# Linear attention and a token mixer in one kernel: mix columns in token order through a stepped matmul operand, and one 256 KB store for each output tile

## The chip, the core and the metric

The kernel runs on one core of a Trainium2 chip. The metric is the device time of one execution in microseconds (us). Before the change three runs took 142.1, 142.66 and 143.6 us; the median is 142.66.

A core has five engines that run side by side, each with its own list of instructions in a fixed order: TensorE (PE; its weight loads are shown as PEld), VectorE (DVE), ScalarE (ACT), GpSimd (POOL) and SyncE (SP). SP issues most DMAs here and ACT a few; 16 DMA engines move the bytes. PE writes only to PSUM (8 banks of 2 KB in each of 128 partitions), and ACT or DVE copies from there to SBUF. In names such as SPq or ACTq the q stands for the engine's sequencer, which waits and issues DMAs.

## The reference: what is computed

Inputs are q, k, v of shape (8, 8, 576, 64) (batches, heads, tokens, head dimension) and three weights, all float32. A linear attention with cosine and sine weights over the positions gives x of shape (8, 576, 512); a mixer over the tokens then gives the output of shape (8, 576, 512) in float32.

```python
r = np.maximum(x, 0.0); phi = np.concatenate([r * c, r * s], axis=-1)   # q_p, k_p
kv = np.einsum('bhsf,bhsd->bhfd', k_p, v);  z = np.sum(k_p, axis=2)
num = np.einsum('bhsf,bhfd->bhsd', q_p, kv)
den = np.einsum('bhsf,bhf->bhs', q_p, z)[..., None] + 1e-06
x = (num / den)                      # heads side by side: (b, s, 512)
wq = x @ w_q;  wk = x @ w_k          # (b, s, 64)
W_tok = scale * np.einsum('bsd,btd->bst', wq, wk)
mixed = np.einsum('bst,btd->bsd', W_tok, x)
out = np.maximum(mixed, 0.0) @ w_out
```

The kernel takes the mixer in another order: it multiplies wk with x first (kx, 64 x 512 for a batch) and then wq with that (mix), so the 576 x 576 matrix W_tok is never made.

## The kernel before

**Layout.** Tokens of a batch lie in SBUF as 64 rows of 9: token t = 9 s + c is at row s and chunk c, which lets a load read long runs. Two head pairs make a "half batch" H, 16 of them; rows 0 to 63 of a tile hold one head of a pair and rows 64 to 127 the other. Everything that is transposed from such tiles has its 576 columns in the order (c, s): 9 blocks of 64. That is the column order of `xT_buf`, of `wT_buf` (rows 0 to 63 wq, rows 64 to 127 wk, the columns after a first block of 64 zeros) and of `wq2`, a copy of wq on rows 64 to 127.

**Stages.** For each H the loads of q, k and v (L250: each a tile `raw` of 128 x 2 x 576 float32, made of two DMAs of 288 KB, one for each head pair), ReLU and cast on POOL (L350, L375), the weighting of k on DVE (L363), transposes of q and their weighting (L385, L391), kv (L399), the numerator and denominator (L424, L428), the division on DVE (L435, L437). For each batch: transposes of x (L449), wq and wk (L464, copied by `wqk_evac`), `wq2` (L475), kx (L494), then mix: four steps j for a batch. Step j = 2 nh + i takes half nh of the tokens and 128-wide part i of each half of the 512 features; it makes two matmuls (L510, `mx_mm`), r = 0 on rows 0 to 63 against `wT_buf`, r = 1 on rows 64 to 127 against `wq2`, into two banks. `mx_evac` (L522 on ACT, L524 on DVE) scales, applies the ReLU and writes 288 columns of `mix_sb` for both.

**Output.** `mix_sb` holds two batches, 1152 columns. Output tile rt (9 for two batches, 36 in all) multiplies 128 of these columns with w_out in four matmuls (L534, `wout_mm`) and is copied to `o_sb` (L337 on ACT, L339 on DVE), one of ten buffers. As the columns are in the order (c, s), 64 columns share one c, and their tokens lie 9 apart: `store` (L544) therefore sends two DMAs of 64 rows of 2 KB, 18 KB apart in memory. `out_dest` computes where each begins.

**Order of work.** `plan_order` lays every operation out ahead of time from a table of costs: it fixes each engine's order and, for copies, which of ACT and DVE makes them. The change does not touch it. SP issues loads and stores in that one order, so that a store which waits for its copy holds back the loads behind it. For the last two batches the second half of tiles 4 to 8 is issued by ACT instead (L617), behind ACT's own copy of that tile.

Of the kernel before, what the change touches and what calls it, by code (L numbers as in the profile page):

```python
# [181 lines left out]
def kernel(  # L182
# [10 lines left out]
    nc = tc.nc  # L193

    B, NH, S, D = q.shape
    DM = NH * D
    DH = moe_w_q.shape[1]
    P = 128
    NPAIR = NH // 2
    C9 = (2 * S) // P  # L200
# [6 lines left out]
    SLOTS = C9 + 1  # L207
    KW = 2 * (D + 1)
    hs = S // 2
# [15 lines left out]
    def bank(i, n=1):  # L225
        return ps[:, i:i + n, :]
# [13 lines left out]
    def load(H, parts=((0, C9),), names=("q", "k", "v"), engs=()):  # L240
        if H >= NB:
            return
        b, h0 = divmod(2 * H, NPAIR)
        for nm in names:
            raw[nm, H] = inp.tile([P, 2, HC], FP32, name="raw")
        for lo, hi in parts:
            for nm in names:
                eng = nc.scalar if lo == 0 and nm in engs else nc.sync
                for i in range(2) if H else (slice(0, 2),):
                    eng.dma_start(raw[nm, H][:, i, lo * D:hi * D],  # L250
                                  srcs[nm][b][:, h0:h0 + 2, lo * D:hi * D][:, i])
# [48 lines left out]
    v_bufs, rq_bufs, qpt_bufs, xT_bufs, wT_bufs = [], [], [], [], []  # L300
# [20 lines left out]
    def load_w(part):  # L321
        if part == 0:
            nc.sync.dma_start(wq_f, moe_w_q.rearrange("(c p) j -> p c j", p=P))
            nc.sync.dma_start(wk_f, moe_w_k.rearrange("(c p) j -> p c j", p=P))
        else:
            nc.sync.dma_start(wo_f, moe_w_out.rearrange("(c p) n -> p c n", p=P))
# [25 lines left out]
    def relu_q(H, lo, hi, eng):  # L352
        relu(rq_bufs[H % 3][:, lo:hi], raw_c("q", H, lo, hi), eng)

    def relu_k(H, lo, hi, eng):
        if lo == 0:
            rks[H] = prep.tile([P, C9, 2, D], BF16, name="rk")
        relu(rks[H][:, lo:hi], raw_c("k", H, lo, hi), eng)

    def mul_k(H, lo, hi):  # L360
        if lo == 0:
            kp[H] = prep.tile([P, 2 * C9, 2, D], BF16, name="kp")
        nc.vector.tensor_mul(  # L363
            kp[H][:, 2 * lo:2 * hi],
            rks[H][:, lo:hi].rearrange("p c i d -> p (c i) d").unsqueeze(2)
            .to_broadcast([P, 2 * (hi - lo), 2, D]),
            cossin[:, 2 * lo:2 * hi])

    def cast_v(H, lo, hi, eng):
        src = raw_c("v", H, lo, hi)  # L370
        dst = v_bufs[H % 3][:, lo:hi, :, 0:D]
        if eng is nc.scalar:
            nc.scalar.copy(dst, src)
        else:
            eng.tensor_scalar(dst, src, 1.0, 1.0, op0=ALU.mult, op1=ALU.mult)  # L375

    xs, kvs, wkjs, wqTs, kxs, mixs = {}, {}, {}, {}, {}, {}

    def half_rows(r):
        return slice(64 * r, 64 * r + 64)  # L380

    def qT_mm(H):
        for c in range(C9):
            for r in range(2):
                nc.tensor.transpose(  # L385
                    bank_h(K0 + r)[:, 0, c * D:(c + 1) * D],
                    rq_bufs[H % 3][half_rows(r), c, :, :],
                    ident[half_rows(r), half_rows(r)])

    def qT_evac(H, r):  # L390
        nc.vector.tensor_mul(  # L391
            qpt_bufs[H % 2][:, r, :, D:SLOTS * D],
            bank_h(K0 + r)[:, 0:1, 0:HC].to_broadcast([P, 2, HC]), cst)

    def kv_mm(H):
        for c in range(C9):
            for i in range(2):
                for r in range(2):
                    nc.tensor.matmul(  # L399
                        bank(K0 + r)[:, 0, i * (D + 1):(i + 1) * (D + 1)],  # L400
                        kp[H][half_rows(r), 2 * c + i, :, :],
                        v_bufs[H % 3][half_rows(r), c, i, 0:D + 1],
                        start=(c == 0 and i == 0), stop=(c == C9 - 1 and i == 1))

    def kv_evac(H, eng):
        kv_sb = small.tile([P, 2, KW], BF16, name="kv_sb")
        kv_sh = small.tile([P, 2, D + 1], BF16, name="kv_sh")
        src = bank(K0, 2)
        copy(eng, kv_sb, src[:, :, 0:KW])
        copy(eng, kv_sh[0:64], src[64:128, :, 0:D + 1])  # L410
        copy(eng, kv_sh[64:128], src[0:64, :, D + 1:KW])
        kvs[H] = (kv_sb, kv_sh)
# [18 lines left out]
    def norm(H, r):  # L431
        b, h = divmod(H, 2)
        nv = bank(N0, 2)[:, :, 0:SC * (D + 1)].rearrange("p t (u e) -> p t u e", u=SC)
        rec = small.tile([P, 2, SC, 1], FP32, name="rec")
        nc.vector.reciprocal(rec, nv[:, :, :, D:D + 1])  # L435
        xv = xs[b].rearrange("p u (h t r) d -> p h r t u d", h=2, r=2)
        nc.vector.tensor_tensor(  # L437
            xv[:, h, r], nv[:, :, :, 0:D], rec.to_broadcast([P, 2, SC, D]), op=ALU.mult)
# [15 lines left out]
    def xT_evac(H, r, m, eng):  # L454
        b, h = divmod(H, 2)
        xv = xT_bufs[b % 2].rearrange("p m (c s) -> p m c s", s=D)
        n = SC - 1 + r
        copy(eng, xv[:, 2 * h:2 * h + 2, 1 - r:C9:2, :],
             bank_h(m)[:, 0, 0:2 * n * D].rearrange("p (m u s) -> p m u s", m=2, u=n))
# [45 lines left out]
    def mx_mm(b, j, m):  # L505
        nh, i = divmod(j, 2)
        for r in range(2):
            rhs = (wT_bufs[b % 2][0:64, D + nh * hs:D + (nh + 1) * hs] if r == 0
                   else wqTs[b][64:128, nh * hs:(nh + 1) * hs])
            nc.tensor.matmul(  # L510
                bank(m + r)[:, 0, 0:hs], kxs[b][half_rows(r), i * P:(i + 1) * P],
                rhs, start=True, stop=True)
# [10 lines left out]
        else:  # L523
            eng.tensor_scalar(dst, src, scale_moe, 0.0, op0=ALU.mult, op1=ALU.max)  # L524

    def out_dest(bp, rt, hi):
        bloc, j0 = divmod(P * rt + 64 * hi, S)
        return (2 * bp + bloc) * S * DM + (j0 // 64) * DM

    o_sbs = {}  # L530

# [7 lines left out]
        o_sbs[bp, rt] = outpool.tile([P, DM], FP32, name="o_sb")  # L539
        copy(eng, o_sbs[bp, rt], bank(m)[:, 0, :])  # L540

    def store(bp, rt, qs):
        for hi in range(2):
            qs[hi].dma_start(  # L544
                dataclasses.replace(out, offset=out.offset + out_dest(bp, rt, hi),
                                    ap=[[C9 * DM, 64], [1, DM]]),
                o_sbs[bp, rt][64 * hi:64 * hi + 64, :])

    A, V, G = nc.scalar, nc.vector, nc.gpsimd
    engs = {"ACT": A, "DVE": V}  # L550
# [7 lines left out]
    def emit(n, eng, m):  # L558
        kind, b, j = n[0], n[1], n[2] if len(n) > 2 else 0
        if kind == "load":  # L560
            load(j, names=(b,))
        elif kind == "load_w":
            load_w(b)
        elif kind == "rq":
            for lo, hi in CS:
                relu_q(b, lo, hi, G)
        elif kind == "rk":
            for lo, hi in CS:
                relu_k(b, lo, hi, G)
        elif kind == "rv":  # L570
            for lo, hi in CS:
                cast_v(b, lo, hi, G)
        elif kind == "mk":
            mul_k(b, 0, C9)
        elif kind == "qT":
            qT_mm(b)
        elif kind == "qe":
            qT_evac(b, j)
        elif kind == "kv":
            kv_mm(b)  # L580
        elif kind == "kve":
            kv_evac(b, engs[eng])
        elif kind == "num":
            num_mm(b, j)
        elif kind == "norm":
            if b // 2 not in xs:
                xs[b // 2] = xpool.tile([P, SC, NH, D], BF16, name="x_sb")
            norm(b, j)
        elif kind == "xT":
            xT_mm(b, m)  # L590
        elif kind == "xe":
            xT_evac(b, j, m, engs[eng])
        elif kind == "wqk":
            wqk_mm(b, m)
        elif kind == "we":
            wqk_evac(b, m, engs[eng])
        elif kind == "wqc":
            wq_copy(b)
        elif kind == "wk":
            wk_mm(b, m)  # L600
        elif kind == "wke":
            wk_evac(b, m, engs[eng])
        elif kind == "kx":
            kx_mm(b, m)
        elif kind == "kxe":
            kx_evac(b, m, engs[eng])
        elif kind == "mx":
            mx_mm(b, j, m)
        elif kind == "mxe":
            mx_evac(b, j, m, engs[eng])  # L610
        elif kind == "wo":
            wout_mm(b, j, m)
        elif kind == "oe":
            wout_evac(b, j, m, engs[eng])
        elif kind == "st":
            last = b == B // 2 - 1 and j >= 4
            store(b, j, (nc.sync, A if last else nc.sync))  # L617
        elif kind == "cw":
            cast_w(b)
        elif kind == "warm":  # L620
            warm_up(b)
# [33 lines left out]
```

## Time and profile before

| what | us |
|---|---|
| median of three runs | 142.66 |
| the profiled execution, its own time | 143.6 |
| its span, first to last instruction | 141.5 |
| PE busy / DVE / ACT / POOL | 113.6 / 94.5 / 78.7 / 74.7 |
| matmuls of the output, L534, 144 of 413 ns | 40.5 |
| matmuls of mix, L510, 64 of about 0.32 | 18.4 |
| stores issued by SP / by ACT, of 128 KB | 67 / 5 |

The kernel reads 29.62 MB from memory and writes 9.44 MB. "Busy" is time in which an engine works; waiting and issuing are not in it. Matmuls are pipelined, so that the duration of one is longer than its distance from the next: where the text needs what a matmul takes from PE, it uses distances in the chain of waits. That chain follows the work that ended last back from the end of the span: start, length and what it was, each step leading to what released it. The granted clock is the share of full speed that PE's clock had. The DMA share is the mean busy share of the 16 DMA engines, and can be slightly above 1.

### The profile page before, as it was taken

What the parts mean: (1) busy time and instruction counts of PE and PEld (TensorE: products, weight loads), DVE (VectorE), ACT (ScalarE), POOL (GpSimd) and SP (SyncE); (2) the same over time, 40 slices, a digit from 0 to 9 for tenths busy, and PEclk for the clock granted to TensorE, in tenths of its full rate; (3) what the DMA queues carried; (4) which work ended last, traced back from release to release, by engine and by line L of the source; (5) the groups of instructions that cost most, each with busy time, mean ns of one, the idle gap of its engine ahead of it and who ended that gap; (6) DMA issues with size and microseconds to landing.
All of it is one profiled execution on the core that took longest, in us unless ns stands there. A gap on an engine that the chain in (4) does not pass through costs nothing.

```text
span 141.5 us, 5415 instructions
## 1 busy us (share of the span) xinstructions
PE 113.6 (80%) x2279; PEld 65.8 (47%) x2279; DVE 94.5 (67%) x153; ACT 78.7 (56%) x154; POOL 74.7 (53%) x121
## 2 busy tenths in 40 slices
PE   5958668676999899689583999599919999989940
PEld 2325346445556456355352466356516575533310
DVE  1166986989929999885959595869468736454400
ACT  6930165377757766675373487466825535745440
POOL 7638978995999988273375545964370000000000
PEclk9999999997589999999999599959985569999996
DMA  3999999999999999999999999989866031755974
GB/s 105 370 390 390 347 373 390 368 390 393 393 390 381 300 324 285 311 315 251 313 337 356 354 351 339 378 275 281 281 200 155 5 74 34 153 116 129 199 215 129
DMA packets 21960, 39.41 MB, mean 279 GB/s; under 512 B 3760, under 2 KB 5296, under 8 KB 21936
## 3 DMA queue, kind: packets, MB, share of 16 engines
q1 hardware_dynamic: 21264, 38.09, 82.3%
q10 hardware_dynamic: 672, 0.98, 2.4%
q8 instruction: 18, 0.29, 0.9%
q14 instruction: 6, 0.05, 0.1%
HBM read 29.62 MB, written 9.44 MB: 276 GB/s over the span
## 4 chain that ended last, share of the span: by engine, by line
DMA 57%; PE 15%; SPq 6%; DVE 6%; POOL 5%; issue 3%; ACT 3%; ACTq 2%; POOLq 0%
DMA raw<-in_k_dram 20%; DMA raw<-in_q_dram 18%; DMA raw<-in_v_dram 8%; DMA out_dram<-o_sb 7%; PE ps L534 7%; SPq L250 5%; DMA wq_f<-in_moe_w_q_dram 4%; POOL rk L350 3%; ACT o_sb L337 2%; DVE qpt_buf L391 2%; PE ps L464 2%; DVE kp L363 2%; ACTq L544 2%; PE ps L424 1%; PE ps L399 1%
## 5 line engine op out<-in xcount | busy, mean ns | idle before, releaser
L534 PE MATMUL ps<-wo_sb,mix_sb 128*128 128x512 bf16 x144 | 40.5, 413 | 0.7 <-ACT o_sb L337 0.5
L363 DVE TENSOR_TENSOR kp<-rk,cossin 128x2304 bf16<-128x2304 bf16 (+2 forms) x17 | 22.4, 1318 | 18.7 <-POOL rk L350 12.7
L375 POOL TENSOR_SCALAR v_buf<-raw 128x640 bf16<-128x640 f32 (+1 forms) x30 | 25.6, 869 | 11.1 <-DMA raw<-in_v_dram 7.8
L350 POOL TENSOR_SCALAR rq_buf<-raw 128x640 bf16<-128x640 f32 (+1 forms) x32 | 25.5, 813 | 10.7 <-DMA raw<-in_q_dram 9.3
L337 ACT COPY o_sb<-ps 128x512 f32<-128x512 f32 x32 | 18.8, 587 | 20.7 <-PE ps L534 13.3
L437 DVE TENSOR_TENSOR x_sb<-ps,rec 128x640 bf16<-128x640 f32 x32 | 26.4, 825 | 1.1
L424 PE MATMUL ps<-kv_sb,qpt_buf 64*128 64x65 bf16 x320 | 16.8, 198 | 10.9 <-DVE x_sb L437 10.8
L424 PEld LDWEIGHTS <-qpt_buf 64*128 64x128 bf16 x640 | 15.0, 98 | 21.3 <-issue 20.2
L350 POOL TENSOR_SCALAR rk<-raw 128x640 bf16<-128x640 f32 (+1 forms) x30 | 19.6, 671 | 9.0 <-DMA raw<-in_k_dram 7.3
L391 DVE TENSOR_TENSOR qpt_buf<-ps,cst 128x1152 bf16<-128x1152 bf16 x32 | 22.6, 748 | 0.0
L534 PEld LDWEIGHTS <-mix_sb 128*128 128x128 bf16 x144 | 12.4, 102 | 15.7 <-issue 5.2
L522 ACT ACTIVATE mix_sb<-ps 128x576 bf16<-128x576 f32 x24 | 14.7, 660 | 6.0 <-PE ps L510 6.0
L399 PE MATMUL ps<-v_buf,kp 64*128 64x65 bf16 x576 | 15.1, 203 | 3.6 <-DVE qpt_buf L391 2.5
L337 ACT COPY xT_buf<-ps 128x640 bf16<-128x640 bf16 (+1 forms) x25 | 15.7, 650 | 3.4 <-PE ps L449 2.2
L424 PE MATMUL ps<-kv_sh,qpt_buf 64*128 64x65 bf16 x320 | 16.8, 197 | 0.9
L399 PEld LDWEIGHTS <-kp 64*128 64x128 bf16 x576 | 12.2, 102 | 8.7 <-issue 3.7
L337 ACT CAST kv_sb<-ps 128x260 bf16<-128x260 f32 x13 | 4.9, 377 | 13.6 <-PE ps L399 13.1
L260 PE MATMUL ps<-warm 128*128 128x512 bf16 x31 | 10.2, 472 | 1.5 <-DVE warm L256 1.5
L510 PE MATMUL ps<-wT_buf,kx 64*128 64x288 bf16 x32 | 9.1, 319 | 2.2 <-ACT mix_sb L522 1.6
L435 DVE RECIPROCAL rec<-ps 128x10 f32<-128x10 f32 x32 | 6.9, 215 | 5.8 <-PE ps L428 5.5
L510 PE MATMUL ps<-wq,kx 64*128 64x288 bf16 x32 | 9.3, 321 | 1.1 <-DVE wq L475 0.8
L464 PE MATMUL ps<-xT_buf,wqk_sb 128*128 128x288 bf16 x64 | 9.9, 301 | 0.0
(51 smaller groups left out, 117.1 us busy)
## 6 DMA issues: line engine op xcount, KB each, us to landing
raw<-in_q_dram SPq DMA_DIRECT2D x30, 288.0 KB, 5.9
raw<-in_k_dram SPq DMA_DIRECT2D x30, 288.0 KB, 5.6
raw<-in_v_dram SPq DMA_DIRECT2D x30, 288.0 KB, 5.6
out_dram<-o_sb SPq DMA_DIRECT2D x67, 128.0 KB, 4.1
wo_f<-in_moe_w_out_dram SPq DMA_DIRECT2D x1, 1024.0 KB, 8.1
out_dram<-o_sb ACTq DMA_DIRECT2D x5, 128.0 KB, 2.8
raw<-in_k_dram ACTq DMA_DIRECT2D x1, 320.0 KB, 4.4
raw<-in_q_dram SPq DMA_DIRECT2D x1, 320.0 KB, 4.1
```

The lines of the kernel that those rows point to most:

```text
L337: nc.scalar.copy(dst, src)
L350: eng.tensor_scalar(dst, src, FMAX, 0.0, op0=ALU.min, op1=ALU.max)
L363: nc.vector.tensor_mul(kp[H][:, 2 * lo:2 * hi], rks[H][:, lo:hi].rearrange("p c i d -> p (c i) d").unsqueeze(2) .to_broadcast([P, 2 * (hi ...
L375: eng.tensor_scalar(dst, src, 1.0, 1.0, op0=ALU.mult, op1=ALU.mult)
L391: nc.vector.tensor_mul(qpt_bufs[H % 2][:, r, :, D:SLOTS * D], bank_h(K0 + r)[:, 0:1, 0:HC].to_broadcast([P, 2, HC]), cst)
L399: nc.tensor.matmul(bank(K0 + r)[:, 0, i * (D + 1):(i + 1) * (D + 1)], kp[H][half_rows(r), 2 * c + i, :, :], v_bufs[H % 3][half_rows(r), c, ...
L424: nc.tensor.matmul(nb[t][:, u, :], qpt_bufs[H % 2][rows, r, w, u * P:(u + 1) * P], mv, start=(u == 0 and w == 0), stop=False)
L437: nc.vector.tensor_tensor(xv[:, h, r], nv[:, :, :, 0:D], rec.to_broadcast([P, 2, SC, D]), op=ALU.mult)
L464: nc.tensor.matmul(bank(m + nh)[:, 0, 0:hs], wqk_sb[:, dmc, :, :], xT_bufs[b % 2][:, dmc, nh * hs:(nh + 1) * hs], start=(dmc == 0), stop=( ...
L510: nc.tensor.matmul(bank(m + r)[:, 0, 0:hs], kxs[b][half_rows(r), i * P:(i + 1) * P], rhs, start=True, stop=True)
L522: nc.scalar.activation(dst, src, AF.Relu, scale=scale_moe)
L534: nc.tensor.matmul(bank(m)[:, 0, :], mixs[bp][:, dmc, rt * P:(rt + 1) * P], wo_sb[:, dmc, :], start=(dmc == 0), stop=(dmc == NDM - 1))
```

## The change

Two things change, and the order on PE, DVE and POOL stays the same instruction by instruction; on SP and ACT only stores go.

The moving operand of the mix matmuls is read in token order: from columns (c, s) it takes, for 32 rows s, the nine chunks c, so that neighbouring columns of the operand lie 64 bf16 elements apart. The 288 columns that come out are 288 tokens in their own order, for nh = 0 the first and for nh = 1 the second half of the batch. `mix_sb`, and with it each output tile, is then in token order.

An output tile is therefore 128 neighbouring rows of the output, 256 KB in one piece, and is stored by one DMA of 128 rows. For the last two batches ACT issues tiles 5 and 7 alone, and SP all others.

```diff
     def mx_mm(b, j, m):
         nh, i = divmod(j, 2)
         for r in range(2):
-            rhs = (wT_bufs[b % 2][0:64, D + nh * hs:D + (nh + 1) * hs] if r == 0
-                   else wqTs[b][64:128, nh * hs:(nh + 1) * hs])
+            rhs = wT_bufs[b % 2][0:64, D:SLOTS * D] if r == 0 else wqTs[b][64:128, :]
+            rhs = rhs.rearrange("j (c s) -> j s c", c=C9)[:, 32 * nh:32 * nh + 32, :]
             nc.tensor.matmul(
                 bank(m + r)[:, 0, 0:hs], kxs[b][half_rows(r), i * P:(i + 1) * P],
                 rhs, start=True, stop=True)
...
-    def out_dest(bp, rt, hi):
-        bloc, j0 = divmod(P * rt + 64 * hi, S)
-        return (2 * bp + bloc) * S * DM + (j0 // 64) * DM
+    rows = out.rearrange("b s d -> (b s) d")
...
-    def store(bp, rt, qs):
-        for hi in range(2):
-            qs[hi].dma_start(
-                dataclasses.replace(out, offset=out.offset + out_dest(bp, rt, hi),
-                                    ap=[[C9 * DM, 64], [1, DM]]),
-                o_sbs[bp, rt][64 * hi:64 * hi + 64, :])
+    def store(bp, rt, eng):
+        r0 = 2 * bp * S + P * rt
+        eng.dma_start(rows[r0:r0 + P, :], o_sbs[bp, rt])
...
             last = b == B // 2 - 1 and j >= 4
-            store(b, j, (nc.sync, A if last else nc.sync))
+            store(b, j, A if last and j % 2 else nc.sync)
```

## The prediction

> **What bounds the kernel now.** I read the page's slices first, then the table of windows, then the chain of waits, then the groups behind single terms. Windows show microseconds, the busy time of PE, PEld, DVE, ACT and POOL with instruction counts, granted clock, DMA share, GB/s.
>
> ```profile
> 12.00:40.00 28.00, 20.93 (x551) 13.74 (x550) 24.08 (x37) 14.49 (x32) 23.92 (x31) 0.88 1.05 381
> 40.00:60.00 20.00, 18.34 (x437) 11.28 (x437) 16.86 (x26) 13.31 (x30) 16.32 (x20) 0.99 0.98 328
> 60.00:80.00 20.00, 15.53 (x349) 9.22 (x349) 15.09 (x27) 10.67 (x20) 10.98 (x17) 0.95 0.97 320
> 80.00:100.00 20.00, 18.10 (x414) 11.05 (x413) 15.39 (x25) 13.12 (x29) 12.39 (x18) 0.88 0.98 325
> ...
> 132.00:137.00 5.00, 3.87 (x18) 1.47 (x16) 0.76 (x1) 2.26 (x4) 0.00 (x0) 1.00 0.87 205
> ...
> 40.00:107.00 67.00, 55.89 (x1298) 34.20 (x1298) 51.11 (x83) 40.05 (x83) 43.19 (x58) 0.93 0.95 314
> 107.30:131.85 24.55, 23.69 (x341) 12.60 (x336) 14.06 (x26) 14.25 (x27) 0.00 (x0) 0.83 0.43 94
> ```
>
> There are three stages. To about 107 us the DMA engines are full, at 381 GB/s before the stores begin and about 324 after. From 107.3 to 131.85 PE is busy 23.69 of 24.55 us. After that ACT empties the last tiles. The chain confirms the first and third stage:
>
> ```profile
> 63.99 1.47 SPq L250
> ...
> 66.04 5.03 DMA out_dram<-o_sb
> ...
> 71.15 0.38 SPq L250
> ...
> 94.09 0.60 SPq L544
> ...
> 130.64 0.23 PE ps L510 x2
> ...
> 131.92 0.59 ACT o_sb L337
> ...
> 132.53 0.55 ACTq L544
> ...
> 133.80 0.76 ACTq L544
> ...
> 137.09 0.59 ACT o_sb L337
> ```
>
> A load's issue at 71.15 was released by the landing of half a store issued at 66.04, so SP's issues and their queue, not only bytes, stand on the chain. In the tail ACT's copies alternate with ACT's own store issues.
>
> **Stores: one issue instead of two.** The row for 40 to 106 us (shortest, median, longest ns):
>
> ```profile
> L544 SPq DMA_DIRECT2D out_dram<-o_sb x42: 472/594/2114, 39.9 to 105.6; - x42
> ...
> L250 SPq DMA_DIRECT2D raw<-in_q_dram x16: 328/436/1471, 41.5 to 95.4; - x16
> ```
>
> 21 of the 42 issues go: 21 x 0.594 = 12.5 us of SP time. SP's order is otherwise kept, so each later load moves past one issue fewer per tile. What arrives at the end is bounded below by 0 (DMA share 0.97 to 0.98: the same bytes remain) and above by the lost rate: 19.46 MB moved in 40 to 100 us take 51.1 us at 381 GB/s, so 8.9 us. I take the part of the chain that is SP issue: its pieces from 54 to 96 us add up to 7.6 us (1.15 + 2.63 + 0.40 + 0.46 + 0.37 + 2.63). Second halves are 12.5 of the 45.9 us that SP's median issues cost there (42 x 0.594 + 48 x 0.437), 27%: 7.6 x 0.27 = 2.1 us. Loads that land earlier are hidden again if PE has no room; it has 67 - 55.9 = 11.1 us.
>
> One rule speaks against this term. The Trainium skill, "DMA: Bandwidth & Descriptors", section "Issuing engines are not separate DMA queues", says that a sequencer's time to start a DMA is usually small beside the transfer. By that alone the 2.1 would be 0 and the whole sum -0.1 instead of -2.2. The row disagrees here: 0.594 us of issue stand beside 128 KB that take 0.34 us at 381 GB/s.
>
> **Stores at the end.** ACT issues two stores (tiles 5 and 7) instead of five halves, and SP the rest. Until the last copy, 0.55 + 0.76 + 0.50 + 0.50 = 2.31 us of ACT's chain are issues; two of about 0.50 stay. The copies then wait for PE, whose twelve matmuls for tiles 5 to 7 run from 132.00 to 134.84, about 0.95 us a tile. Copy 4 ends at 132.51, copy 5 at 133.55, its store issue at 134.1, copy 6 at 134.7, copy 7 at 135.4, its issue at 136.0, copy 8 at 136.6; before it ended at 137.68. That is -1.1 us; a little less if the banks of tiles 6 and 7 keep PE waiting longer, but not above 0, since issues only go. The last store goes out as one DMA on SP. ACT's halves landed a median 2.8 us after issue, SP's 2.4 in that window; the half that is now added costs up to 0.36 us (128 KB at 363 GB/s, which is 381 over its share of 1.05), so the landing is between 0 and 0.4 us earlier: I take 0.2. The 64-row halves move 205 / 0.87 = 236 GB/s per full share in the tail; that more is possible with 128 rows covers this 0.2.
>
> **The strided moving operand.** The order of instructions on PE, DVE and POOL stays as it was; 64 matmuls change their read. Columns are now taken with a step of 64 bf16 elements, 9 at a time. No matmul before has such a step in a long moving operand, so its price is bounded from neighbours:
>
> ```profile
> 123.00 0.98 PE ps L464 x8
> 123.97 0.27 PE ps L510 x2
> ...
> L510 PE MATMUL ps<-wT_buf,kx x32: 279/288/444, 30.3 to 131.8; 64*128 64x288 bf16 x32
> ```
>
> Eight contiguous 288-column matmuls take 0.98 us, 0.12 each. A mix pair, its two halves on different rows of the array and side by side, takes 0.23 to 0.27; so about 0.12 is streaming and the rest a change of mode. Below: nothing added (a gain has no source, columns and instructions are the same). Above: 0.36 a pair, if the two no longer run side by side and each also takes twice its 0.12 (4 x 0.12 instead of 0.12). I take a doubling of the stream, 0.12 a pair, since the nearest rows of a slower stream are those at half clock: 444 ns at most against 279, 0.165 more.
>
> The Trainium skill warns of this read: "SBUF — State Buffer", section "Door 1: The DMA port swizzle", holds that SBUF is read at full rate only with two or more accesses to each 16-byte line, and a 128-byte step has one. It gives no factor for a matmul, and no run here shows it yet. Without its penalty the sum would be -3.4 instead of -2.2.
>
> Of the 32 pairs the windows of that line put 4 before 40 us, 16 between 40 and 107, 4 between 107 and 120 and 8 between 120 and 132. The last twelve lie where PE is the bound. Eight run at full clock: 8 x 0.12 = 1.0 us. Four lie in the stretch whose mean clock is 0.68, where a slower read may disappear under the slower array: half price, 0.2. So +1.2. The 16 of the middle cost 1.9 us in PE's 11.1 us of idle time there; without that cover they are 1.9 more. The four of the start lie under loads. Where a mix copy on ACT or DVE gets its bank 0.12 later, what waits is the next output tile in PE's own order, which is already counted.
>
> **Sum.** -2.1 - 1.1 - 0.2 + 1.2 = -2.2 us. The profiled execution took 143.6 us, 2.1 of them around a span of 141.5; it would take 141.4 with a span of 139.3. It was the slowest of three runs; on their median of 142.66 the forecast is 140.5.
>
> **Rivals.** (a) Slower: the step costs more than a doubling, and PE's idle time in the middle is no room for it, being mostly waits for DVE's normalisation (10.8 us in 8 waits), which itself follows PE. With half of the 16 middle pairs exposed, 20 pairs count. The other terms give 3.4 us, so the point from which it decides is 3.4 / 20 = 0.17 us a pair; at the upper bound of 0.36 it is 7.2 - 3.4 = +3.8: 146.5. For it: every column is a step. Against: no row shows a stream slowed more than about twice. (b) The DMA engines bind the middle whatever SP does: share 0.97 and more. Then -1.1 - 0.2 + 1.2 = -0.1: 142.6, no change. (c) The step costs nothing: -3.4, 139.3. (d) The load stream regains half of its lost rate, 4.5 us, because a store takes one place instead of two in the queue that the load at 71.15 waited on: -4.5 - 1.3 + 1.2 = -4.6, 138.1. For it: 381 GB/s before the stores and 324 after, at hardly any change of share. Against: the same bytes are still written between the loads.
>
> **Numbers.** Forecast 0.34, (a) 0.20, (b) 0.17, (c) 0.17, (d) 0.12. The range 137.6 to 144.8 takes in all centres but that of (a), of which the lower half is inside; outside are its upper half and a third of (d). The forecast's own range is 139 to 142.5. A measurement can tell about 1% here: 141.2 and 144.1. Faster by more: two thirds of the forecast 0.22, (c) 0.16, (d) 0.12: 0.50. Within: the rest of the forecast 0.11, (b) 0.15 and 0.01 of (c): 0.27. Slower: (a) and the rest of (b), 0.22, and 0.01 of the forecast: 0.23.
>
> **What would show it.** In the changed profile: 34 store issues on SP instead of 67 and two on ACT instead of five; GB/s in 40 to 100 us above 324 and the last load's landing about 2 us earlier; mix pairs at 0.35 instead of 0.23 in the chain; the last copy about 1.1 us nearer to the last matmul. The forecast is wrong if the pair costs 0.5 or more, or if PE's pause before 107 us closes and its clock of 0.68 does not return.

## The result, and the profile after

The changed kernel took 135.15 us (median of 4 runs, 135.11 to 135.99) against 142.5 for the kernel before (4 runs, 142.1 to 143.6): a ratio of 0.949 with an interval of 0.942 to 0.955. The forecast was 140.5 with a range from 137.6. The direction is right; the gain is 7.3 us where 2.2 were forecast, and the time lies below the range.

The runs of the kernel before scatter by themselves, from 137.3 to 146.3 us over the 49 taken for this study (median 142.0), and the ratios are formed from the runs near each kernel's fastest, so that a ratio and a pair of medians can differ by one or two per cent. A second comparison (six new runs of the changed kernel, eleven of the one before) gave medians of 135.4 and 141.2 and a ratio of 0.974 (0.961 to 0.986). The two intervals do not meet: the kernel is faster both times, and how much faster is known only as some 4 to 7 us.

The table of windows of the changed kernel, with the columns of the prediction (busy time of PE, PEld, DVE, ACT and POOL, granted clock, DMA share, GB/s):

```profile
12.00:40.00 28.00, 21.88 (x551) 13.20 (x550) 24.02 (x37) 14.45 (x32) 23.64 (x31) 0.91 1.06 382
40.00:60.00 20.00, 20.00 (x435) 11.62 (x434) 15.47 (x24) 12.39 (x28) 18.01 (x24) 0.96 1.05 400
60.00:80.00 20.00, 18.92 (x389) 10.25 (x388) 17.52 (x30) 13.24 (x25) 13.41 (x19) 0.91 1.04 388
80.00:100.00 20.00, 19.32 (x465) 11.79 (x458) 17.44 (x30) 14.85 (x32) 11.30 (x16) 1.00 0.72 266
100.00:107.00 7.00, 6.89 (x182) 4.32 (x183) 6.29 (x11) 4.89 (x11) 0.00 (x0) 1.00 0.17 59
107.00:120.00 13.00, 12.44 (x174) 5.90 (x166) 6.39 (x14) 7.57 (x15) 0.00 (x0) 1.00 0.28 104
```

The last two stretches in the kernel before:

```profile
100.00:107.00 7.00, 3.92 (x104) 2.65 (x103) 3.76 (x6) 2.96 (x7) 3.50 (x5) 0.87 0.74 227
107.00:120.00 13.00, 12.78 (x247) 7.85 (x242) 8.37 (x16) 7.12 (x16) 0.00 (x0) 0.68 0.25 55
```

Read the last column first. Until 40 us, before the first store, both kernels move 381 or 382 GB/s. From then on the kernel before fell to 328 and 320; the changed one rises to 400 and 388. Its last load has landed at 93.3 us instead of 104.5. PE, which had nothing to do for 3.1 of 7 us between 100 and 107 us and then ran at a clock of 0.68, is now busy throughout at 1.00.

The bound has moved with it. The chain's shares by engine in the page of the changed kernel:

```profile
PE 62%; DMA 14%; DVE 10%; POOL 4%; ACT 4%; issue 2%; SPq 1%; POOLq 0%; ACTq 0%
```

and in that of the kernel before:

```profile
DMA 57%; PE 15%; SPq 6%; DVE 6%; POOL 5%; issue 3%; ACT 3%; ACTq 2%; POOLq 0%
```

Where DMAs made up most of the chain, matmuls do now: PE is busy for 116.7 of a span of 132.9 us. The chain of waits of the changed kernel shows what they cost (start, length, what):

```profile
47.14 0.58 PE ps L510 x2
...
120.35 0.58 PE ps L510 x2
120.93 0.97 PE ps L532 x4
...
123.47 0.57 PE ps L510 x2
124.04 0.98 PE ps L532 x4
...
125.09 0.59 ACT o_sb L337
...
125.70 2.02 DMA out_dram<-o_sb
127.72 0.57 ACT o_sb L337
...
128.34 1.04 PE ps L532 x4
...
129.40 0.59 ACT o_sb L337
```

A mix pair (L510) takes 0.57 to 0.58 us where it took 0.23 to 0.27, while four matmuls of an output tile, now in L532, take 0.97 as before. The line of the mix matmuls (shortest, median, longest ns) says the same of a single one:

```profile
L510 PE MATMUL ps<-wT_buf,kx x32: 638/641/662, 30.6 to 124.9; 64*128 64x288 bf16 x32
```

641 ns stand against 288. The stores, from the view of the output tensor:

```profile
L542 SPq DMA_DIRECT2D out_dram<-o_sb x34: 332/343/855, 40.0 to 130.0; - x34
L542 ACTq DMA_DIRECT2D out_dram<-o_sb x2: 338/346/354, 127.2 to 128.9; - x2
...
DMA to landing us min/median/max: 2.0/4.3/5.7
```

An issue of 128 rows takes 343 ns; one of 64 rows took 594.

### The profile page after: what moved, and what is told of

Its sections match the earlier page's. It is cut to its first block, busy times and chain, and to the rows that moved or that the text cites. A ratio compares the mean times of both kernels' runs of the same rounds, so it can differ in the third digit from the quotient of the medians.

```text
span 132.9 us, 5368 instructions
## 1 busy us (share of the span) xinstructions
PE 116.7 (88%) x2279; PEld 63.2 (48%) x2279; DVE 94.4 (71%) x153; ACT 79.1 (60%) x154; POOL 74.1 (56%) x121
## 2 busy tenths in 40 slices
DMA packets 21384, 39.41 MB, mean 297 GB/s; under 512 B 3184, under 2 KB 4720, under 8 KB 21360
## 4 chain that ended last, share of the span: by engine, by line
PE 62%; DMA 14%; DVE 10%; POOL 4%; ACT 4%; issue 2%; SPq 1%; POOLq 0%; ACTq 0%
PE ps L532 25%; PE ps L510 10%; PE ps L424 7%; PE ps L464 6%; PE ps L399 5%; DMA raw<-in_q_dram 5%; DMA raw<-in_k_dram 4%; DMA raw<-in_v_dram 4%; PE ps L494 3%; DVE kp L363 3%; PE ps L449 3%; PE ps L385 2%; DVE qpt_buf L391 2%; POOL rk L350 2%; POOL rq_buf L350 2%
## 5 line engine op out<-in xcount | busy, mean ns | idle before, releaser
L532 PE MATMUL ps<-wo_sb,mix_sb 128*128 128x512 bf16 x144 | 39.0, 402 | 0.0
L375 POOL TENSOR_SCALAR v_buf<-raw 128x640 bf16<-128x640 f32 (+1 forms) x30 | 24.6, 836 | 6.4 <-DMA raw<-in_v_dram 3.5
L350 POOL TENSOR_SCALAR rq_buf<-raw 128x640 bf16<-128x640 f32 (+1 forms) x32 | 22.2, 711 | 8.3 <-DMA raw<-in_q_dram 5.7
L350 POOL TENSOR_SCALAR rk<-raw 128x640 bf16<-128x640 f32 (+1 forms) x30 | 23.3, 794 | 5.2 <-DMA raw<-in_k_dram 4.9
L424 PEld LDWEIGHTS <-qpt_buf 64*128 64x128 bf16 x640 | 14.9, 96 | 13.4 <-issue 12.6
L510 PE MATMUL ps<-wT_buf,kx 64*128 64x288 bf16 x32 | 19.6, 644 | 1.9 <-ACT mix_sb L522 1.0
L532 PEld LDWEIGHTS <-mix_sb 128*128 128x128 bf16 x144 | 12.1, 101 | 17.6 <-issue 7.8
L510 PE MATMUL ps<-wq,kx 64*128 64x288 bf16 x32 | 19.6, 643 | 0.0
L399 PE MATMUL ps<-v_buf,kp 64*128 64x65 bf16 x576 | 12.9, 192 | 3.1 <-DVE qpt_buf L391 2.1
L399 PEld LDWEIGHTS <-kp 64*128 64x128 bf16 x576 | 10.8, 95 | 8.8 <-issue 4.4
L337 ACT CAST kv_sb<-ps 128x260 bf16<-128x260 f32 x13 | 4.9, 376 | 11.9 <-PE ps L399 11.7
L524 DVE TENSOR_SCALAR mix_sb<-ps 128x576 bf16<-128x576 f32 x8 | 6.1, 756 | 6.8 <-PE ps L510 5.1
L260 PE MATMUL ps<-warm 128*128 128x512 bf16 x31 | 9.2, 432 | 1.5 <-DVE warm L256 1.5
```

The source lines that it names most:

```text
L260: nc.tensor.matmul(bank(M3)[:, 0, :], warm[:, 0:P], warm, start=True, stop=True)
L350: eng.tensor_scalar(dst, src, FMAX, 0.0, op0=ALU.min, op1=ALU.max)
L399: nc.tensor.matmul(bank(K0 + r)[:, 0, i * (D + 1):(i + 1) * (D + 1)], kp[H][half_rows(r), 2 * c + i, :, :], v_bufs[H % 3][half_rows(r), c, ...
L424: nc.tensor.matmul(nb[t][:, u, :], qpt_bufs[H % 2][rows, r, w, u * P:(u + 1) * P], mv, start=(u == 0 and w == 0), stop=False)
L510: nc.tensor.matmul(bank(m + r)[:, 0, 0:hs], kxs[b][half_rows(r), i * P:(i + 1) * P], rhs, start=True, stop=True)
L532: nc.tensor.matmul(bank(m)[:, 0, :], mixs[bp][:, dmc, rt * P:(rt + 1) * P], wo_sb[:, dmc, :], start=(dmc == 0), stop=(dmc == NDM - 1))
```

## Experiments

Each kernel is the changed one with the edit shown. Rates are GB/s in the windows 40 to 60 and 60 to 80 us, where both kernels have loads and stores mixed.

### Which part of the change does it

**Two halves again.** The stepped operand stays; a tile leaves as two DMAs of 64 neighbouring rows.

```diff
-        eng.dma_start(rows[r0:r0 + P, :], o_sbs[bp, rt])
+        for hi in range(2):
+            eng.dma_start(rows[r0 + 64 * hi:r0 + 64 * hi + 64, :],
+                          o_sbs[bp, rt][64 * hi:64 * hi + 64, :])
```

> The changed kernel with every tile stored as two DMAs of 64 neighbouring rows (128 KB each, both on the queue that issued the one). Theory H (halves: what slowed the loads before was that a tile went out as two 64-row DMAs): the middle falls back to about 324 GB/s between 40 and 100 us, the last load lands near 104 us instead of 93, and with the dearer mix matmuls on top the time is 142 to 147 us. Theory A (apart: it was the 18 KB between rows in memory): the middle stays near 390 GB/s, the last load lands near 93 us, and the time is 135 to 137 us; only SP's issues double.

Measured: 144.91 us, ratio to the kernel before 1.035 (1.024 to 1.046). Its table of windows:

```profile
40.00:60.00 20.00, 18.76 (x429) 11.17 (x432) 16.69 (x25) 13.27 (x30) 18.25 (x23) 1.00 1.02 365
60.00:80.00 20.00, 18.64 (x345) 10.30 (x349) 16.15 (x29) 11.60 (x22) 11.31 (x16) 0.83 0.97 319
```

and its store issues on SP, in the view of the output tensor:

```profile
L543 SPq DMA_DIRECT2D out_dram<-o_sb x68: 466/537/1448, 40.1 to 140.0; - x68
```

The 68 issues take a median 537 ns each, the rate is lost again, and PE's clock is 0.83 from 60 to 80 us. The kernel is 9.8 us slower than the changed one: all of the gain hangs on the single store.

**Plain operand.** The store stays single; the mix matmuls read neighbouring columns as before, so that the rows of the output come out in the order (c, s).

```diff
-            rhs = wT_bufs[b % 2][0:64, D:SLOTS * D] if r == 0 else wqTs[b][64:128, :]
-            rhs = rhs.rearrange("j (c s) -> j s c", c=C9)[:, 32 * nh:32 * nh + 32, :]
+            rhs = (wT_bufs[b % 2][0:64, D + nh * hs:D + (nh + 1) * hs] if r == 0
+                   else wqTs[b][64:128, nh * hs:(nh + 1) * hs])
```

> The changed kernel with the mix matmuls reading contiguous columns as before, so that the rows of the output land in the order (c, s); the work and the stores are those of the changed kernel. Theory P (PE is the bound from about 35 us on): 28 of the 32 pairs lie there, 0.35 us dearer each, so 9.8 us come off: 125 to 127 us. Theory Q (loads gate PE until they end at 93 us, and only the 12 pairs behind them count): 4.2 us come off: 130 to 132 us, and PE shows the idle time of the others as waits.

Measured: 129.89 us, ratio 0.930 (0.920 to 0.940), 390 and 378 GB/s. The single store alone is therefore worth 7% of the kernel before, about 10 us by the ratio and 12.5 by the medians, and the stepped operand takes 135.15 - 129.89 = 5.3 of it back. PE's busy time tells the same from its side: 105.0 us here and 116.7 with the step, 11.7 more, which is about 32 pairs of 0.36 (23 of the 2279 matmul records are missing here). Somewhat under half of that reaches the end. Whether the step costs less where loads set the pace is not settled: the kernel with two halves, which has the step, lies 2.5 us above the kernel before by the medians and 5 by the ratio.

### What the second DMA of a tile costs

**The rows' distance in memory.** One DMA of 128 rows, as far apart (18 KB) as in the halves of the kernel before; the rows of the output land in another order.

```diff
-        r0 = 2 * bp * S + P * rt
-        eng.dma_start(rows[r0:r0 + P, :], o_sbs[bp, rt])
+        eng.dma_start(
+            dataclasses.replace(out, offset=out.offset + (2 * bp * S + rt) * DM,
+                                ap=[[C9 * DM, P], [1, DM]]),
+            o_sbs[bp, rt])
```

> The changed kernel with one 128-row DMA for each tile as now, but to rows 18 KB apart in memory (tile rt writes rows rt, rt + 9, ... of its two batches, so the rows of the output land in another order). Theory H: as the changed kernel, 135 to 136 us, 390 GB/s in the middle. Theory A: load packets are slowed as before, 324 GB/s in the middle, last load near 104 us, 142 us and more.

Measured: 135.65 us, ratio 0.961 (0.942 to 0.980), 388 and 376 GB/s: about the changed kernel's time. That the 256 KB are in one piece, which the change brings about, is worth nothing that shows.

**Another cut.** Two DMAs of all 128 rows, each with half of the columns:

```diff
+        for hi in range(2):
+            cols = slice(hi * DM // 2, (hi + 1) * DM // 2)
+            eng.dma_start(rows[r0:r0 + P, cols], o_sbs[bp, rt][:, cols])
```

> The changed kernel with each tile stored by two DMAs of 128 rows, each with half of the columns (1 KB a row, 128 KB in all), so that the number of DMAs is that of the two 64-row halves and the rows are all 128. Theory R (rows: a 64-row DMA itself slows the loads around it): 135 to 138 us, about 390 GB/s in the middle. Theory N (number: two issues and two places in the queue for a tile starve the DMA engines): as the 64-row halves, 143 to 146 us, 330 GB/s in the middle.

and two of 64 rows, the even and the odd ones, so that each reaches over all 128 partitions:

```diff
+        for hi in range(2):
+            eng.dma_start(
+                rows[r0:r0 + P, :].rearrange("(p two) d -> two p d", two=2)[hi],
+                o_sbs[bp, rt][hi:P:2, :])
```

> The changed kernel with each tile stored by two DMAs of 64 rows of 2 KB, the even rows and the odd rows of the tile, so that each spreads over all 128 rows of SBUF instead of the lower or the upper half. Theory S (side: what hurts is that a DMA stays on one half of the rows of SBUF): 135 to 138 us and about 390 GB/s. If 64 rows hurt whatever their place, or if the number does (theory N): 143 to 146 us and 330 GB/s.

Measured: 141.27 us for the columns, ratio 0.999 (0.992 to 1.006), 355 and 330 GB/s; 145.44 for even and odd rows, ratio 1.035 (1.020 to 1.050), 336 and 307 GB/s. That a DMA of 64 rows stays on one half of the rows of SBUF is not what costs the rate. Two DMAs lose it in each of the three cuts.

**Who issues.** Two halves, the lower issued by SP and the upper by ACT, so that SP has as many store issues as in the changed kernel.

```diff
+        for hi, q in ((0, nc.sync), (1, nc.scalar)):
+            q.dma_start(rows[r0 + 64 * hi:r0 + 64 * hi + 64, :],
+                        o_sbs[bp, rt][64 * hi:64 * hi + 64, :])
```

> The changed kernel with each tile stored as two 64-row DMAs, the lower half issued by SP and the upper half by ACT for every tile. SP then issues as many DMAs as in the changed kernel, the DMA engines get the same 72 halves as with both on SP, and ACT issues about 36 times 0.5 us more. Theory I (SP's issue time and its queue of landings are what slows the loads): the middle recovers to 375 GB/s or more, the last load lands before 97 us, and the time is 136 to 140 us, with what ACT loses in it. Theory E (the 64-row transfers themselves hold up the DMA engines): 325 to 340 GB/s in the middle and 143 us or more.

Measured: 148.12 us, ratio 1.049 (1.035 to 1.063). The windows:

```profile
40.00:60.00 20.00, 17.35 (x352) 9.85 (x350) 13.52 (x21) 10.09 (x21) 15.95 (x22) 0.89 1.00 344
60.00:80.00 20.00, 15.58 (x274) 8.14 (x270) 12.91 (x23) 9.68 (x20) 10.85 (x16) 0.91 0.94 301
```

ACT now has issues between its copies, so the time can have losses of its own; the rate is what counts here, and it does not come back. To take half of the store issues off SP, whose issue time the forecast built on, is not enough; what SP waits for instead is shown below.

**How many DMAs, and how large.** Another limit shows in SP's timeline of the kernel before, at the point of the chain that the prediction quoted (start, length, what was issued):

```profile
66.04 1.11 SPq L544 DMA_DIRECT2D out_dram<-o_sb  x2
67.25 1.01 SPq L250 DMA_DIRECT2D raw<-in_k_dram  x2
68.36 1.29 SPq L544 DMA_DIRECT2D out_dram<-o_sb  x2
70.04 1.01 SPq L250 DMA_DIRECT2D raw<-in_v_dram  x2
71.15 0.86 SPq L250 DMA_DIRECT2D raw<-in_q_dram  x2
```

The store of 66.04 landed at 71.07, and that released the load of 71.15. Eight DMAs lie from the one to the other. In the trace the landings are counted on eight semaphores used in turn, by SP's and ACT's DMAs together, so an issue waits until the DMA eight places before it has landed. If that is the limit, what counts is how many bytes fill eight places. A store of 128 KB takes a place that a load of 288 KB could have.

The same lines show how close this limit lies to the other one. SP's issue before the load of 71.15 ended at 71.05, only 0.02 us before the landing, and SP leaves about 0.1 us between any two issues: the wait cost it next to nothing. Of the 5.01 us from 66.04 to 71.05 it issued for 4.4. Both limits, places and SP's own time, ease when there are fewer DMAs. Three kernels change the number of DMAs in other ways: loads as one DMA of 576 KB with single stores, the same with two halves, and loads as four DMAs with single stores.

```diff
-                for i in range(2) if H else (slice(0, 2),):
+                for i in (slice(0, 2),):
```

```diff
                 for i in range(2) if H else (slice(0, 2),):
-                    eng.dma_start(raw[nm, H][:, i, lo * D:hi * D],
-                                  srcs[nm][b][:, h0:h0 + 2, lo * D:hi * D][:, i])
+                    for e0, e1 in ((0, 5), (5, C9)) if H else ((lo, hi),):
+                        eng.dma_start(raw[nm, H][:, i, e0 * D:e1 * D],
+                                      srcs[nm][b][:, h0:h0 + 2, e0 * D:e1 * D][:, i])
```

> The changed kernel with each load as one DMA of 576 KB, the control for the kernel before it. The middle is near 390 GB/s already, so under both theories the loads end near 93 us; POOL may start a tile later, as nothing lands before all of it: 134.5 to 137 us.

> The kernel with two 64-row stores a tile and the stepped mix read (144.9 us), with each load of q, k or v made as one DMA of 576 KB instead of two of 288. The stores are untouched; the number of DMAs in the middle falls by a third. Theory B (few bytes on the way: an issue waits for the landing of the DMA eight places before it, and small DMAs in these places leave the engines too little to do): the places now hold more, the middle recovers to 370 GB/s or more, the last load lands before 98 us, 136 to 139 us. Theory E (each 64-row store itself costs the DMA engines time): the middle stays at 320 to 340 GB/s and the time at 143 to 146 us.

> The changed kernel with each load of q, k or v made as four DMAs of 128 rows (five or four chunks of each head pair, 160 or 128 KB) instead of two; stores stay one DMA of 128 rows. No DMA has 64 rows. Theory B: eight places hold half as many bytes (about 1.2 MB instead of 2.3), the middle falls to 340 GB/s or less, the last load lands after 102 us, 141 us and more. Theory E: no 64-row store is there, so the middle stays above 375 GB/s and the time is 135 to 138 us.

Measured: 135.64 us (ratio 0.966, 0.936 to 0.995), 139.19 (0.984, 0.960 to 1.008) and 161.4 (1.151, 1.137 to 1.166). The windows of the kernel with loads in four:

```profile
40.00:60.00 20.00, 16.89 (x291) 8.93 (x290) 11.23 (x17) 13.99 (x30) 13.09 (x17) 0.77 0.88 266
60.00:80.00 20.00, 14.33 (x297) 8.16 (x297) 12.70 (x22) 8.68 (x17) 11.24 (x17) 0.83 0.93 288
```

With the same single store the rate is now far below that of the kernel before, at a DMA share of 0.88 to 0.93. All kernels together, ordered by the mean size of a DMA. For one half batch 1728 KB are loaded and 576 KB stored (36 tiles over 16 half batches), and the size is 2304 KB over the number of DMAs; the rate is the mean of the two windows. The last column adds up the lengths of SP's issues from 40 to 80 us.

| kernel | DMAs per half batch | KB each | GB/s | SP issuing, us of 40 |
|---|---|---|---|---|
| loads in four, single store | 12 + 2.25 | 162 | 277 | 34.1 |
| before; and two halves in the four ways above | 6 + 4.5 | 219 | 324; 342, 342, 322, 322 | 33.1; 32.6, 29.8, 32.6, 21.5 |
| changed, rows apart, plain operand | 6 + 2.25 | 279 | 394, 382, 384 | 23.3, 23.2, 23.5 |
| one load, two halves | 3 + 4.5 | 307 | 370 | 27.7 |
| one load, single store | 3 + 2.25 | 439 | 390 | 19.7 |

The rate rises with the size up to about 280 KB and then stays between 370 and 394. That number and size of the DMAs decide is shown by the pairs that keep the rows of each DMA as long as they were: two halves against the single store, and one load against two. The loads in four also read shorter rows (packets under 2 KB go from 4720 to 29200), which was not tested apart.

Which of the two limits holds in which kernel can be read from SP's timeline. In the kernel with loads in four SP issues with no more than its usual 0.1 us in between:

```profile
61.23 1.80 SPq L251 DMA_DIRECT2D raw<-in_v_dram  x4
63.13 2.97 SPq L251 DMA_DIRECT2D raw<-in_q_dram  x4
66.20 0.38 SPq L543 DMA_DIRECT2D out_dram<-o_sb  x1
66.67 2.82 SPq L251 DMA_DIRECT2D raw<-in_k_dram  x4
```

In the changed kernel it stands still for 1.65 us before the first store here and for 0.82 before the second:

```profile
63.26 0.97 SPq L250 DMA_DIRECT2D raw<-in_q_dram  x2
65.88 0.34 SPq L542 DMA_DIRECT2D out_dram<-o_sb  x1
66.31 0.88 SPq L250 DMA_DIRECT2D raw<-in_k_dram  x2
68.01 0.34 SPq L542 DMA_DIRECT2D out_dram<-o_sb  x1
```

From 40 to 80 us the pauses of more than 0.2 us add up to 3.2 us in the kernel before, 3.7 with two halves and 1.2 with loads in four, but to 14.9 in the changed one, where 30 of 33 end as the DMA eight places before lands. So where the rate is low SP issues nearly all the time, and places seldom hold it up; places hold it up in the changed kernel. They also do where ACT issues half of the stores: SP pauses for 16.8 us there, 16.2 of them until such a landing, and the rate stays low. Taking away one limit uncovers the other. How much of the 10 us belongs to each stays open, since no kernel here changed the number of places or the issue time alone. Nor does a run show why issues also grew longer: a load's took 0.58 us on average in the kernel before and 0.44 in the changed one, and 0.33 at the shortest in both.

Halves of 64 rows seem to cost a little more than that. Two halves of 64 rows are slower by 3.6 us than two column halves (144.91 against 141.27), and with loads in one DMA by 3.5 than the single store (139.19 against 135.64), though there the number differs too. Their issue takes 0.54 us against 0.39 for the column halves. The intervals of the second pair overlap, and row count and issue time were not parted: that share stays open.

### The stepped operand

**Runs of two and of four columns.** The moving operand keeps the step but takes two or four neighbouring bf16 columns at each place, so that columns come out in another order. One run of each.

```diff
-            rhs = rhs.rearrange("j (c s) -> j s c", c=C9)[:, 32 * nh:32 * nh + 32, :]
+            rhs = rhs.rearrange("j (c s t) -> j s c t", c=C9, t=2)[
+                :, 16 * nh:16 * nh + 16, :, :]
```

> The changed kernel with the stepped moving operand read in runs of two neighbouring elements (4 bytes) instead of single ones; columns land in another order, the work is the same. Theory L (what costs is each new place in SBUF, so half as many places cost half): a mix matmul shows about 400 ns instead of 641 (279 when contiguous). Theory M (any step but one costs the same): 641 ns again. By time: about 131 to 133 us under L, 135 under M.

> The changed kernel with the moving operand read in runs of four neighbouring elements (8 bytes); columns land in another order. Contiguous 279 ns, runs of two 400, single elements 641: the excess over contiguous is 0, 121 and 362, as if each new place took four columns' time. If that is the rule, a run of four costs nothing: 280 ns and 129 to 131 us. If half of the excess remains again: 340 ns.

Measured: 131.83 and 130.76 us. The matmul's line with runs of two:

```profile
L511 PE MATMUL ps<-wT_buf,kx x32: 398/400/425, 30.4 to 122.0; 64*128 64x288 bf16 x32
```

and with runs of four:

```profile
L511 PE MATMUL ps<-wT_buf,kx x32: 279/282/425, 31.1 to 121.0; 64*128 64x288 bf16 x32
```

641, 400, 282 ns, where neighbouring columns take 279 at best. 288 columns stream in 0.12 us, so the excess is three streams, one stream, none: every new place costs the time of four columns, and four columns of bf16 fill that time.

**Pay on DVE.** The copy that makes `wq2` puts the columns into token order, once for each half of the array, and the matmuls read plain columns.

```diff
-        nc.vector.tensor_copy(wq2[64:128], wT_bufs[b % 2][0:64, D:SLOTS * D])
+        src = wT_bufs[b % 2][0:64, D:SLOTS * D].rearrange("j (c s) -> j s c", c=C9)
+        for r in (0, 1):
+            nc.vector.tensor_copy(
+                wq2[half_rows(r)].rearrange("j (s c) -> j s c", c=C9), src)
...
+            rhs = wqTs[b][half_rows(r), nh * hs:(nh + 1) * hs]
```

> The changed kernel with the reordering moved off PE: DVE copies wq in token order for both row halves (two copies of 64 x 576 with a stepped read in place of one contiguous copy), and the mix matmuls read contiguous columns; the output is the reference's. Theory P: PE loses 9.8 us and DVE gains 8 copies of 0.5 to 0.8 us, of which DVE (71% busy) passes on a part: 127 to 131 us. Theory Q: 131 to 134 us. If a stepped read slows DVE as it slows PE (four times, 1.2 to 1.8 us a copy), 16 such copies cost up to 20 us of DVE and the time is 135 us or more.

Measured: 138.55 us, ratio 0.988 (0.977 to 0.999), at an undisturbed 390 and 363 GB/s. The group in its page:

```profile
L477 DVE COPY wq<-wT_buf 64x576 bf16<-64x576 bf16 x16 | 13.5, 842 | 1.2 <-ACT wT_buf L337 1.0
```

16 copies of 842 ns take the place of 8 of 449 in the kernel before. That is 9.9 us more on DVE, which is then busy for 104.4 us, and the kernel is 3.4 us slower than the changed one, which pays 11.7 us on PE.

**Pay where `mix_sb` is written.** Plain operand of 320 or 256 columns; the copies out of PSUM write with a step of nine columns, and an output tile is planned behind all four mix steps of its batch.

```diff
+            c0, c1 = ((0, 5), (5, C9))[nh]
...
+        dst = mixs[b // 2].rearrange("p (r i) n -> p r i n", r=2)[
+            :, :, i, (b % 2) * S:(b % 2 + 1) * S].rearrange(
+            "p r (s c) -> p r c s", c=C9)[:, :, c0:c1, :]
```

> A version meant to keep both gains: the mix matmuls read contiguous columns (five or four whole chunks instead of half of the columns, 320 or 256), and the copy of mix out of PSUM writes them in token order (a step of 9 bf16 elements in SBUF); tiles are stored by one DMA of 128 rows. An output tile now needs all four mix steps of its batch, and the plan is made with that. The output is the reference's. If a stepped write costs ACT and DVE nothing: mix copies stay near 0.65 and 0.76 us and the time is 129 to 132 us. If it slows them as the stepped read slowed DVE's copy (842 against about 450 ns): 32 copies of 0.4 us more on ACT and DVE, 133 to 138 us.

Measured: 195.63 us, ratio 1.394 (1.383 to 1.405). Of its copies:

```profile
L527 ACT ACTIVATE mix_sb<-ps 128x640 bf16<-128x640 f32 x13 | 38.6, 3090 | 1.6 <-PE ps L511 1.6
```

3.09 us for 640 columns, where the changed kernel writes 576 in 0.65. The same copies on DVE took a median 2.96 us. This write with a step cost far more than the read with one above, though its source, float32 in PSUM, was another too.

### A tile that is a chunk

What the single store needs is 128 rows in one DMA, not that they are neighbours. So the tile can be chunk c of two batches, which are 64 columns from each; the copies write runs of 64 columns and nothing is stepped.

```diff
+            c0, c1 = ((0, 5), (5, C9))[nh]
+            rhs = (wT_bufs[b % 2][0:64, D + c0 * D:D + c1 * D] if r == 0
+                   else wqTs[b][64:128, c0 * D:c1 * D])
...
+        dst = mixs[b // 2].rearrange("p (r i) (c b s) -> p r i c b s", r=2, c=C9, b=2)[
+            :, :, i, c0:c1, b % 2, :]
...
+            dataclasses.replace(out, offset=out.offset + (2 * bp * S + rt) * DM,
+                                ap=[[C9 * DM, P], [1, DM]]),
```

The planner is told that an output tile needs mix columns of both batches.

> A second version meant to keep both gains: mix matmuls read contiguous columns (five or four whole chunks), the copy of mix writes runs of 64 columns into the order (chunk, batch, row), so that output tile rt is chunk rt of two batches: 128 rows of the output 9 apart, stored by one DMA of 128 rows. A tile now needs both batches of its pair, so the plan puts nine tiles instead of five behind the last mix step. The output is the reference's. Expected 129 to 133 us: 130 as the kernel with the plain read, and up to 3 us for PE's waits before the last mix step, which fewer tiles fill. Above 135 if those waits cost more than the stepped read did.

Measured: 132.69 us (132.17 to 133.03), ratio 0.942 (0.936 to 0.949), 375 and 379 GB/s; PE is busy for 107.1 us. It was then run again beside the changed kernel:

> The changed kernel, unaltered, beside the version with a chunk of two batches as output tile, on one chip: 135 to 136 us.

> The version in which output tile rt is chunk rt of two batches, unaltered: 132 to 133 us, some 2.5 us under the changed kernel, with intervals that do not overlap if the gain is real.

Measured: 135.39 (133.65 to 138.7) and 132.89 us (131.83 to 134.82), ratios of 0.974 (0.961 to 0.986) and 0.957 (0.945 to 0.968). It beats the kernel before, and its median is 2.5 us below the changed kernel's both times; the intervals of the two ratios still overlap a little, so that is likely and not settled.

## Why the prediction was right and wrong

- **"Stores: one issue instead of two", -2.1 us: this step failed, by its size.** It took 27% of the 7.6 us that the chain of waits puts down to SP's issues from 54 to 96 us. Measured alone, the single store is worth 10 to 12.5 us, of which the end, forecast apart, has about 2. The chain was the wrong measure: it gives a stretch to whatever ended last, so the 5.03 us from 66.04 count as a DMA, though SP issued for 4.4 of them and was done 0.02 us before the landing. SP's issues in fact fill 33.2 of these 42 us. So far more of the 12.5 us of issues that the prediction found to go could reach the loads, and the last load landed 11 us earlier, not 2.
- **Rival (d)** named the other limit, a place in the queue for each store. Its 4.5 us were about half of what came: the load stream regained all of its lost rate. The run with half of the issues on ACT shows that this limit is real, as the rate stayed low while SP waited for landings. How the gain divides between the two limits stays open.
- **The reading under both: "the DMA engines are full".** It rested on a share of 0.97 to 0.98, from which came the doubt about (d) and all of rival (b). The share was no sign of a full rate: the kernel with loads in four shows 0.93 at 288 GB/s, the changed one 1.04 at 388. The fall from 381 to 324 GB/s, quoted in the same fence, was the sign. The Trainium skill, "Perfetto Trace Analysis", section "Identifying the Most-Contended Engine", warns that with 16 DMA engines occupancy is misleading and asks for HBM utilization, a rate, instead; the two rows agree.
- **The rule it set aside.** The Trainium skill, "DMA: Bandwidth & Descriptors", section "Issuing engines are not separate DMA queues", says that starting DMAs on several engines saves only the sequencer's time, and that this is usually small. The prediction took the 0.594 us row to speak against it, and SP's timeline bears that out: issues filled 33.1 of its 40 us. The run with ACT's issues fits the rule's other half: issuing elsewhere gained no rate. That the 2.1 would be 0 by this rule did not follow, since the rule is about who issues and the change is about how many.
- **The stepped operand, +1.2 us: a mis-sized term.** A doubling of the stream, 0.12 a pair, was taken; the pair costs about 0.35 more. That is the upper bound, but reached in another way, which was luck: the bound had two matmuls one after the other at twice the time, and measured were two side by side at four times (641 ns each, 0.57 for the pair). It came to +5.3 us. The count was too low as well: twelve pairs were put on the path, and the chain of the changed kernel, in which PE is the bound from about 35 us on, runs through 24. "No row shows a stream slowed more than about twice" was true of the rows and no reason. The rule of the Trainium skill, "SBUF — State Buffer", section "Door 1: The DMA port swizzle", that two accesses to a 16-byte line give the full rate was right in direction. Taken as two bf16, they are too few here: runs of two still took 400 ns, and four were needed.
- **The condition against it.** "The forecast is wrong if the pair costs 0.5 or more, or if PE's pause before 107 us closes and its clock of 0.68 does not return": all of it happened. The errors of the two terms, some 6 to 8 us of gain and 4 of loss, have opposite signs. That the sum missed by only 5 us is luck.
- **The end, -1.1 and -0.2: the copies as forecast, the landing better.** From the first output matmul behind the last mix pair to the end of the last copy the kernel before took 5.68 us (132.00 to 137.68) and the changed one 4.47 (125.52 to 129.99): 1.2 nearer. From the last copy to the landing of the last store it took 2.80 and 2.02 us, so this part gained 0.8 and not 0.2. The stores are 34 on SP and 2 on ACT, as counted.
- **Rival (a)** had the right price for the pair and the wrong surroundings: 20 pairs at 0.36 would have made the kernel slower, had the store not freed far more than 3.4 us.

## What to carry to other kernels

When transfers of different sizes share one line of issues, look at whether the issuing engine ever pauses, at how many bytes the places in flight can hold, and at the rate before and after the small ones begin; a busy share near 1 hides the loss, and so can the chain of waits. Cut such a stream into few, large DMAs, and do not pay for neighbouring addresses that the transfer does not need: rows 18 KB apart went as fast. Where an order has to be changed on the way, move runs of four bf16 (8 bytes), which cost nothing here, through a matmul's moving operand, and do not let the copies write single bf16 elements with a step, which cost far more here than the step on PE.

## What the runs showed of the hardware

- The number of DMAs costs time at equal bytes: loads cut in four (162 KB a DMA on average) lowered the rate to 277 GB/s and took 26 us more than the changed kernel; SP issued for 34.1 of 40 us.
- A matmul's moving operand in bf16, 288 columns: 279 ns in one run, 282 in runs of four, 400 in runs of two, 641 with every column 128 bytes from the last.
- ACT writing 640 bf16 columns with a step of 18 bytes: 3.09 us; DVE copying 576 read with a step: 842 ns against 449.
- An issue of a 64-row store took 0.54 to 0.59 us, of a 128-row store with twice the bytes 0.34.
- PE's granted clock was 0.68 from 107 to 120 us in the kernel before, behind a pause of 3.1 in 7 us, and 1.00 in that stretch of the changed kernel, which has no such pause.
